# Key weight loads on ScalarE's queue, tile 0 in two halves, tiles 2 and 3 as two loads: one change at the start of a linear-attention and MLP kernel

## The chip, the cores and the metric

The kernel runs on one core of a Trainium2 chip. The metric is the device time of one execution in microseconds (us), the median over several executions. Engines are named as in the profile: PE is TensorE's matmul side and PEld its weight loads, DVE is VectorE, ACT is ScalarE, POOL is GpSimd, SP is SyncE. SPq, ACTq and POOLq are the sequencers of these engines, where waits and DMA issues are recorded.

## The reference: what is computed

The input x has 2048 tokens of 512 channels. It is normalised per token without scale or shift, and the result feeds two branches, which are added to x:

```
xn = (x - mean(x)) / sqrt(var(x) + 1e-5)            # per token, over 512 channels
q, k, v = xn @ wqkv, split in 3, 32 heads of 16     # wqkv is 512 x 1536
pq, pk = phi(q), phi(k)                             # phi(t) = (t + 1 if t > 0 else exp(t)) + 1e-6
kv = sum over tokens of pk^T v ;  z = sum over tokens of pk
o = (pq kv) / (pq . z + 1e-6)
h = relu(xn @ w1 + b1) ** 2                         # w1 is 512 x 1376
out = x + o @ wo + h @ w2 + b2
```

All data are float32. The kernel splits every operand of a product into a high part in a reduced float32 format (fp32r) and the rest, and adds three products (high by high, high by rest, rest by high), so each product of two matrices is three passes of matmuls.

## The kernel before: tiles, stages and order of the work

The 2048 tokens are 16 tiles of 128. The kernel is written with a hand-made schedule: the order of the instructions on each engine is the order in which the program text emits them. Each engine takes its own instructions in that order, and waits only on semaphores.

Three stages follow each other. First, for every tile, the tile is normalised, turned (channels onto partitions), split, and multiplied by the key part of wqkv; phi of that, multiplied by the tokens themselves, is added up over all tiles in four banks (`kx`, line 398). Then comes the queries' part with the small matrices made from that sum. Then the MLP, mixed with the rest of the attention, in two rounds of two blocks of 512 tokens.

The change touches the first few microseconds of stage one. What the code does there:

- Line 69 asks for ScalarE's table of functions (the table load). Lines 517 to 520 run 11 matmuls on a constant, which the profile shows as 22. They use no input.
- Lines 522 to 530 issue the loads, all on SP's queue, in this order: tile 0 (256 KB), tile 1 (256 KB), the four blocks of the key weights `rk` (256 KB each, `load_k`, line 527), and one load of tiles 2 and 3 together (512 KB).
- `statistics` and `measure` (lines 228 to 238) give mean and variance of a tile by `bn_stats` and `bn_aggr` on DVE. `roots` (lines 240 to 244) makes an estimate of the inverse root from a logarithm and an exponential on ACT. `normalise` (lines 246 to 276) refines it in three small instructions on DVE and writes the normalised tile `xp` (line 271).
- In DVE's order the statistics of tiles 0 and 1 both stand ahead of `normalise` of tile 0 (lines 568 to 578).
- `turned_pe` (line 318) transposes a tile by four matmuls; for tiles 0 and 1 the result lies in two halves. `high` (line 334, ACT) and `low` (line 337, DVE) split it into `xs1h` and `xs1l`.
- `heads_k` (line 560) copies a block of key weights into its high part `wkh` on ACT, and `rests_k` (line 564) makes the rest `wkl` on DVE or POOL. On ACT the order is: block 0, first half of tile 0's split, block 1, the other three halves, blocks 2 and 3.
- `some` and `rest` multiply tiles 0 and 1 by the key weights, a block at a time (lines 571 to 622); all of that is recorded at line 379. Tile 2 is measured, normalised and turned behind it (lines 606 to 620), and tile 3 is measured at line 617.
- Lines 586 and 587: a copy of one column on POOL into tile 4's buffer, from a result of tile 1's `normalise`, holds back the load of tiles 4 to 7 (1024 KB) until that result is there.

Of the kernel before, what the change touches and what calls it, by code (L numbers as in the profile page):

```python
# [13 lines left out]
P = 128  # L14
# [4 lines left out]
def kernel(  # L19
# [29 lines left out]
    nc = tc.nc  # L49
    xf = x.rearrange("b s d -> (b s) d")  # L50
    of = out.rearrange("b s d -> (b s) d")
    S, D = xf.shape
# [12 lines left out]
    FL = F - (NF - 1) * P  # L65
    Q = P // TB
    assert D == 512 and S % BT == 0 and FL == 3 * Q

    nc.scalar.preload_act_table_set("natural_log_exp_and_others")

    keep = ctx.enter_context(tc.tile_pool(name="keep", bufs=1))
    work = ctx.enter_context(tc.tile_pool(name="work", bufs=1))
# [12 lines left out]
    def next_tag(of):  # L85
        k, n = turns[of]
        turns[of][0] = (k + 1) % n
        return f"{of}{k}"

    def two(name):  # L90
        return keep.tile([P, 2, 512], F32, name=name, tag=next_tag("x"))

    def four(name, tag, dt=F32, pool=None):
        return (pool or work).tile([P, TB, 512], dt, name=name, tag=tag)
# [38 lines left out]
    def both(name, tags, dt=F32R, pool=keep):  # L133
        return [pool.tile([P, NJ, D], dt, name=f"{name}{u}", tag=t) for u, t in zip("hl", tags)]
# [18 lines left out]
    xr, xp, xg, tok, pk, kp = {}, {}, {}, {}, {}, {}  # L153

    def load_x(i, t):
        n = t.shape[1]
        nc.sync.dma_start(t, xf[i * P:(i + n) * P, :].rearrange("(i p) d -> p i d", i=n))  # L157
        for k in range(n):
            xr[i + k] = t[:, k]
# [6 lines left out]
    def chunk(w, j, a, b):  # L166

        return w[j * P:(j + 1) * P, a:b]
# [59 lines left out]
    def measure(g, *ks):  # L228

        tiles, st, mv, _ = g  # L230
        for k in ks or range(len(tiles)):
            nc.vector.bn_stats(st[:, k, :], xr[tiles[k]])
            nc.vector.bn_aggr(mv[:, k, :], st[:, k, :])

    def statistics(*tiles):
        g = group(*tiles)
        measure(g)
        return g
# [281 lines left out]
        nc.tensor.matmul(pw[:, :P], lhsT=zeros, rhs=zeros, start=True, stop=True)  # L520
    nc.vector.memset(eps, 1e-5)
    t, rk = two("x0"), four("rk", "r0")
    for i in range(2):
        load_x(i, t[:, i:i + 1])
    def load_k(*js):
        for j in js:
            nc.sync.dma_start(rk[:, j], chunk(wqkv, j, D, 2 * D))  # L527

    load_k(*range(NJ))
    load_x(2, two("x2"))  # L530
    nc.gpsimd.memset(ident, 0.0)
    nc.gpsimd.affine_select(out=ident, in_=ident, compare_op=OP.not_equal, fill=1.0, base=0,
                            pattern=[[-1, P]], channel_multiplier=1)
# [8 lines left out]
    for i0 in range(0, NT, TB):  # L542
# [5 lines left out]
        n = TB if i0 >= NPE else NPE - NDVE  # L548
        o = work.tile([P, n, 512], F32, name=f"xg{i0}", tag="r0" if i0 + TB == NT else "r3" if i0 >= NPE else "rc")
        for k in range(0, n, 2):  # L550
            i = i0 + TB - n + k
# [6 lines left out]
    def heads_k(*js, eng="act"):  # L558
        for j in js:
            copy(eng, wk[0][:, j, :], rk[:, j])  # L560
# [7 lines left out]
    two_tiles = statistics(0), statistics(1)  # L568
# [14 lines left out]
    normalise(*two_tiles[1])  # L583
    heads_k(1)

    nc.gpsimd.tensor_copy(x4[:, 0, :1], two_tiles[1][3][:, 2, :1])
    load_x(4, x4)
    low()
# [39 lines left out]
    soon = group(4, 6, 7)  # L628
    phi_k(0, pks[0])
    measure(soon, 0)  # L630
    tokens(0)
    parts(0)
    keep2()
    roots(*fourth)
    normalise(*fourth)
    phi_k(1, pks[1])
    measure(soon, 1)
    tokens(1)
    parts(1)
# [171 lines left out]
    m = both("m", ("mh", "ml"), pool=work)  # L811
# [25 lines left out]
    for n in range(2):  # L837
        t1, t2 = NB - 1 - 2 * n, NB - 2 - 2 * n
        x1, x2 = xsb
# [361 lines left out]
```

## Time and profile before

| what | value |
|---|---|
| median of the runs | 421.64 us (421.62 to 423.54, three runs) |
| the profiled execution's own time | 422.41 us |
| its span, first to last instruction | 420.7 us |
| PE busy | 414.1 us, 98% |
| DVE, ACT, POOL busy | 304.9, 253.0, 55.2 us |
| granted TensorE clock | 0.999 |

A row of the timeline gives the start, the duration, the engine, the line, the operation with output and inputs, and in brackets the idle time of the engine before it with what ended that idle time. Several like instructions in a row are merged into one row with their count. Matmuls are pipelined: one of 512 columns is shown with 0.39 us, while the next one starts 0.23 us after it.

### The profile page before, as it was taken

The numbers are of one execution on the slowest core, as the hardware profiler recorded it, in microseconds if no ns is written. First come the engines' busy times: TensorE is split into PE (matmuls) and PEld (weight loads), VectorE is DVE, ScalarE is ACT, GpSimd is POOL, SyncE is SP. The second block draws the span as 40 slices with busy tenths as digits, with TensorE's granted clock in tenths as the row PEclk, the third lists the DMA queues.
The fourth block names the chain that finished last, engine by engine and source line by source line (L and its number), as shares of the span: only waits on it lengthen the run. The fifth ranks groups of instructions, "written<-read, shape, count | busy, mean of one in ns | idle before, by whom it ended". The sixth has DMA issues, their size and how long they took to land.

```text
span 420.7 us, 5470 instructions
## 1 busy us (share of the span) xinstructions
PE 414.1 (98%) x1859; PEld 340.6 (81%) x1859; DVE 304.9 (72%) x555; ACT 253.0 (60%) x451; POOL 55.2 (13%) x78
## 2 busy tenths in 40 slices
PE   7999999999999999999999999999999999999996
PEld 6788888888887788888888887888788888888875
DVE  5995767786679987777579397586977667577293
ACT  5767777675467777565466371666677665546140
POOL 3231222220004000110000061001000200000240
PEclk9999999999999999999999999999999999999999
DMA  6885423800511322695026676501121784023742
GB/s 235 274 234 163 130 92 99 277 25 3 125 50 52 99 64 63 191 184 175 0 69 190 192 230 159 139 0 50 44 82 26 225 172 153 2 94 87 193 77 100
DMA packets 49485, 50.69 MB, mean 120 GB/s; under 512 B 8241, under 2 KB 33585, under 8 KB 49202
## 3 DMA queue, kind: packets, MB, share of 16 engines
q1 hardware_dynamic: 47154, 46.16, 36.4%
q0 software_dynamic: 2304, 4.20, 6.1%
q8 instruction: 14, 0.23, 0.3%
q14 instruction: 13, 0.11, 0.1%
HBM read 37.23 MB, written 8.91 MB: 110 GB/s over the span
## 4 chain that ended last, share of the span: by engine, by line
PE 96%; DMA 2%; DVE 1%; SPq 1%; issue 0%
PE acc L129 36%; PE b L489 23%; PE kx L398 10%; PE pq L379 10%; PE pk L379 9%; PE acc L500 2%; DMA x<-in_A_x_dram 2%; PE pz L129 1%; PE b L129 1%; PE pkv L820 1%; PE pm L129 1%; PE pt L318 0%; PE acc L507 0%; SPq L527 0%; SPq L157 0%; PE end L129 0%
## 5 line engine op out<-in xcount | busy, mean ns | idle before, releaser
L129 PE MATMUL acc<-w2r,s 128*128 128x512 f32 x477 | 112.8, 389 | 0.0
L129 PEld LDWEIGHTS acc<-w2r,s 128*128 128x128 f32 x477 | 89.5, 188 | 18.9 <-issue 0.2
L489 PE MATMUL b<-T,aop 128*128 128x512 f32 x240 | 59.9, 390 | 0.0
L489 PEld LDWEIGHTS b<-T,aop 128*128 128x128 f32 x240 | 44.8, 188 | 9.8 <-issue 0.5
L398 PE MATMUL kx<-pk,tok 128*128 128x512 f32 x192 | 46.8, 393 | 0.0
L398 PEld LDWEIGHTS kx<-pk,tok 128*128 128x128 f32 x192 | 35.6, 188 | 8.0 <-DVE pk L387 0.6
L956 POOL DMA_DIRECT2D res<-in_B_b_dram x16 | 14.1, 1067 | 150.5 <-DMA res<-in_A_x_dram 57.5
L121 DVE TENSOR_TENSOR w2r<-r,w2r 128x512 fp32r<-128x512 f32 (+2 forms) x35 | 25.4, 725 | 7.3 <-ACT w2r L110 7.2
L129 PE MATMUL acc<-mh,aTsr 128*128 128x512 f32 x96 | 30.6, 391 | 0.0
L118 POOL TENSOR_TENSOR tok<-xp,tok 128x512 fp32r<-128x512 f32 x16 | 21.7, 1363 | 54.8 <-ACT tok L110 54.8
L110 ACT ACTIVATE w2r<-r 128x512 fp32r<-128x512 f32 x32 | 20.0, 625 | 13.7 <-PE acc L129 11.3
L489 PE MATMUL b<-xs0h,aop 128*128 128x512 f32 x80 | 26.4, 391 | 0.0
L118 DVE TENSOR_TENSOR s<-c,s 128x512 fp32r<-128x512 f32 x20 | 13.8, 692 | 15.0 <-ACT s L110 14.9
L110 ACT ACTIVATE aop<-S 128x512 fp32r<-128x512 f32 x20 | 12.6, 629 | 16.1 <-DVE S L749 12.3
L374 DVE SCALAR_TENSOR_TENSOR q<-pq,q 128x512 f32<-128x512 f32 x16 | 11.0, 690 | 14.4 <-ACT q L372 14.4
L129 PEld LDWEIGHTS acc<-mh,aTsr 128*128 128x128 f32 x96 | 18.0, 188 | 4.0 <-issue 0.2
L370 ACT ACTIVATE q<-pq 128x512 f32<-128x512 f32 x16 | 9.4, 590 | 18.6 <-PE pq L379 18.5
L129 PE MATMUL acc<-ml,aTsr 128*128 128x512 f32 x48 | 18.7, 390 | 0.0
L964 DVE TENSOR_TENSOR res<-acc,res 128x512 f32<-128x512 f32 x16 | 11.0, 692 | 9.9 <-PE acc L129 6.6
L489 PEld LDWEIGHTS b<-xs0h,aop 128*128 128x128 f32 x80 | 15.0, 188 | 3.4 <-ACT rz L477 0.3
L303 DVE STREAM_TRANSPOSE at<-g 128x512 f32<-128x512 f32 x16 | 10.4, 689 | 7.9 <-DMA g<-q 7.9
L489 PE MATMUL b<-xs0l,aop 128*128 128x512 f32 x40 | 15.6, 390 | 0.0
(208 smaller groups left out, 854.9 us busy)
## 6 DMA issues: line engine op xcount, KB each, us to landing
r<-in_B_w_dram SPq DMA_DIRECT2D x49, 256.0 KB, 3.1
res<-in_A_x_dram SPq DMA_DIRECT2D x8, 512.0 KB, 5.8
res<-in_B_b_dram POOLq DMA_DIRECT2D x16, 256.0 KB, 5.3
g<-q SPq DMA_DIRECT2D x64, 64.0 KB, 2.5
out_dram<-res SPq DMA_DIRECT2D x15, 256.0 KB, 2.1
x<-in_A_x_dram SPq DMA_DIRECT2D x5, 512.0 KB, 6.0
via<-xp SPq DMA_DIRECT2D x5, 512.0 KB, 2.7
xg<-via SPq DMA_DIRECT2D x20, 128.0 KB, 2.9
```

The source lines that it names most:

```text
L110: nc.scalar.activation(o, i, AF.Copy, bias=bias)
L118: ENG[el].tensor_tensor(out=l, in0=src, in1=f32(h), op=OP.subtract)
L121: nc.vector.tensor_tensor(out=l, in0=src, in1=f32(h), op=OP.subtract)
L129: nc.tensor.matmul(ps, lhsT=a[u], rhs=b[v], start=first and n == 0, stop=last and n == 2)
L303: nc.vector.transpose(o.rearrange("p j (r t) -> p r j t", r=NJ), G.rearrange("p r (j c) -> p r j c", j=NJ))
L370: nc.scalar.activation(p, ps, AF.Relu, scale=-1.0)
L374: nc.vector.scalar_tensor_tensor(p, ps, 0.0, p, op0=OP.max, op1=OP.add)
L379: nc.tensor.matmul(ps, lhsT=cols(i)[u][:, j, slot(i)], rhs=w[v][:, j, :], start=first and n == 0, stop=last and n == len(steps) - 1)
L398: nc.tensor.matmul(kxp[c], lhsT=tok[i][:, u, c * P:(c + 1) * P], rhs=pk[i][:, v], start=i == 0 and (u, v) == first, stop=i == NT - 1 and ( ...
L489: nc.tensor.matmul(ps, lhsT=a[u][:, j * P:(j + 1) * P], rhs=b[v][:, j, :], start=first and j == 0 and n == 0, stop=last and j == 1 and n == 2,
L956: nc.gpsimd.dma_start(r[:, i], b2[None, :].partition_broadcast(P), accum_op=OP.add)
L964: nc.vector.tensor_tensor(out=r[:, a:z], in0=ps, in1=r[:, a:z], op=OP.add)
```

## The change

Four things are altered. Tile 0 is loaded by two loads, 256 of its 512 channels each, and its statistics are taken in two halves, which `bn_aggr` combines. Tile 2 is loaded alone, directly behind tile 1 on SP's queue. The four key weight loads are issued by ScalarE, behind the table load in its order; the call for the table load moves from the top of the function to that place. Tile 3 becomes a load of its own, held back by a second one-column copy on POOL in the same manner as tiles 4 to 7, and stands ahead of them on SP's queue. The `measure` helper is shared by all tiles; only tile 0 takes its branch with two halves.

```diff
-    nc.scalar.preload_act_table_set("natural_log_exp_and_others")
...
         for k in ks or range(len(tiles)):
-            nc.vector.bn_stats(st[:, k, :], xr[tiles[k]])
-            nc.vector.bn_aggr(mv[:, k, :], st[:, k, :])
+            n = 1 if tiles[k] else 2
+            for m in range(n):
+                nc.vector.bn_stats(st[:, k + m, :], xr[tiles[k]][:, m * D // n:(m + 1) * D // n])
+            nc.vector.bn_aggr(mv[:, k, :], st[:, k:k + n, :])
...
     t, rk = two("x0"), four("rk", "r0")
-    for i in range(2):
-        load_x(i, t[:, i:i + 1])
+    for k in range(2):
+        at = slice(k * D // 2, (k + 1) * D // 2)
+        nc.sync.dma_start(t[:, 0, at], xf[:P, at])
+    xr[0] = t[:, 0]
+    x2 = two("x2")
+    load_x(1, t[:, 1:])
+    load_x(2, x2[:, :1])
     def load_k(*js):
         for j in js:
-            nc.sync.dma_start(rk[:, j], chunk(wqkv, j, D, 2 * D))
+            nc.scalar.dma_start(rk[:, j], chunk(wqkv, j, D, 2 * D))
+    nc.scalar.preload_act_table_set("natural_log_exp_and_others")
     load_k(*range(NJ))
-    load_x(2, two("x2"))
...
     normalise(*two_tiles[1])
     heads_k(1)
 
+    nc.gpsimd.tensor_copy(x2[:, 1, :1], two_tiles[1][3][:, 2, :1])
+    load_x(3, x2[:, 1:])
     nc.gpsimd.tensor_copy(x4[:, 0, :1], two_tiles[1][3][:, 2, :1])
     load_x(4, x4)
```

## The prediction

> **What bounds the kernel now.** I read the page first, then the busy time by stretch, then the chain of work that ended last, and last the timeline of the first 13 us.
>
> ```profile
> span 420.7 us, 5470 instructions
> PE 414.1 (98%) x1859; PEld 340.6 (81%) x1859; DVE 304.9 (72%) x555; ACT 253.0 (60%) x451; POOL 55.2 (13%) x78
> ```
> ```profile
> 5.00:13.07 8.07, 5.92 (x28) 4.54 (x29) 6.82 (x23) 5.66 (x17) 1.65 (x4) 1.00 0.79 274
> 13.07:21.00 7.93, 7.92 (x38) 6.19 (x39) 7.03 (x16) 6.59 (x14) 2.65 (x4) 1.00 0.90 281
> 21.00:416.00 395.00, 395.00 (x1765) 324.93 (x1764) 288.20 (x512) 239.08 (x420) 49.34 (x63) 1.00 0.41 113
> ```
>
> The second fence gives, per stretch, its length and then the busy time of PE, PEld, DVE, ACT and POOL, the granted clock, the DMA share and GB/s. From 13.07 us on PE is never without work (395.00 of 395.00 us), at full clock. So a change to the start is worth exactly the shift of the moment from which PE runs unbroken, here the transposes of tile 2 at 13.07, as long as nothing later is made late. Ahead of it PE lacks 2.15 of 8.07 us. The chain shows what that moment hangs on:
>
> ```profile
> 3.62 6.65 DMA x<-in_A_x_dram
> ...
> 10.29 0.71 DVE st L232
> ...
> 13.07 0.63 PE pt L318 x4
> ```
> ```profile
> 8.35 0.40 PE L379 MATMUL pk<-wkh,xs1h 128*128 128x512 f32 x1
> ...
> 12.02 0.39 PE L379 MATMUL pk<-wkh,xs1h 128*128 128x512 f32 x1
> 12.25 0.39 PE L379 MATMUL pk<-wkh,xs1l 128*128 128x512 f32 x1
> 13.07 0.63 PE L318 MATMUL pt<-ident,xp 128*128 128x128 f32 x4 [0.44 <-DVE xp L271]
> ```
>
> The load of tiles 2 and 3 is issued seventh, lands 6.65 us later, and DVE measures tile 2 only then. Matmuls start 0.23 us apart (12.02, 12.25), so PE could have gone on at 12.48: the wait costs 13.07 - 12.48 = 0.59 us. That is all the gap at tile 2 can give back. The rest of the missing 2.15 us lies ahead of 8.35, where PE waits for tile 0 and the first key block:
>
> ```profile
> 0.81 1.28 ACT L69 ACT_TABLE_LOAD   x1 [0.81 <-PEq L1187]
> 0.81 0.87 SPq L157 DMA_DIRECT2D x<-in_A_x_dram  x2
> 1.72 1.85 SPq L527 DMA_DIRECT2D rk<-in_A_wqkv_dram  x4
> 3.59 0.69 DVE L232 BATCH_NORM_STATS2 st<-x 128x6 f32<-128x512 f32 x1 [2.65 <-DMA x<-in_A_x_dram]
> 4.32 0.18 DVE L233 BATCH_NORM_AGGREGATE mv<-st 128x2 f32<-128x6 f32 x1
> 4.42 0.66 DVE L232 BATCH_NORM_STATS2 st<-x 128x6 f32<-128x512 f32 x1
> 4.54 0.29 ACT L243 ACTIVATE y<-mv,eps 128x1 f32<-128x1 f32 x1 [2.45 <-DVE mv L233]
> 6.08 0.63 ACT L110 ACTIVATE wkh<-rk 128x512 fp32r<-128x512 f32 x1 [0.22 <-DMA rk<-in_A_wqkv_dram]
> 6.46 0.63 PE L318 MATMUL pt<-ident,xp 128*128 128x128 f32 x4 [1.52 <-DVE y L252]
> 6.90 0.39 ACT L334 ACTIVATE xs1h<-pt 128x256 fp32r<-128x256 f32 x1 [0.19 <-PE pt L318]
> 7.18 0.62 ACT L110 ACTIVATE wkh<-rk 128x512 fp32r<-128x512 f32 x1
> 8.51 1.09 DVE L337 TENSOR_TENSOR xs1l<-pt,xs1h 128x256 fp32r<-128x256 f32 x3 [0.17 <-ACT xs1h L334]
> ```
>
> ACT copies key block 0 at 6.08, when it lands; the first split of tile 0 stands behind that copy, at 6.90.
>
> **Part 1, tile 0 in halves.** Two issues for one, two statistics for one. One `bn_stats` of 512 takes 0.69; a half is an estimate of 0.42, since DVE's `xs1l` takes 1.09 for three of 256. Both loads' bytes are those of the one load, so I keep 3.56 us for the last of them. The second half is then measured by 4.0, not 4.28, and the aggregate is 0.27 earlier. It is not on the path: in DVE's order tile 1's statistics come before line 252, and tile 1 is now the third issue, not the second, 0.47 later.
>
> ```profile
> x<-in_A_x_dram SPq DMA_DIRECT2D x1, 256.0 KB, 2.8
> rk<-in_A_wqkv_dram SPq DMA_DIRECT2D x1, 256.0 KB, 4.3
> DMA to landing us min/median/max: 4.3/4.7/5.9
> x<-in_A_x_dram SPq DMA_DIRECT2D x1, 512.0 KB, 6.6
> x<-in_A_x_dram SPq DMA_DIRECT2D x1, 1024.0 KB, 7.1
> ```
>
> These rows are issue to landing: tile 0, key block 0, all four key blocks, tiles 2 and 3, and tiles 4 to 7. Tile 1, issued near 1.25, lands near 4.1 if it takes tile 0's 2.8; it waited then for tile 0's bytes more than for its issue. After, it lands between 4.1 and 4.6, and its statistics, at 4.42 before, start between 4.2 and 4.65. I take 4.42, the middle: 0 us, with -0.2 and +0.25 as ends.
>
> **Part 2, the key loads on ACT.** Four issues leave SP; ACT gets four. Nothing in this trace shows ACT issuing a load. The nearest row is SP's 0.43 per issue (1.85 for four with gaps); the far one is POOL's:
>
> ```profile
> L956 POOL DMA_DIRECT2D res<-in_B_b_dram x16: 844/940/1529, 176.9 to 401.0; - x16
> ```
>
> I take SP's, since these are plain loads as SP's are. If they start where the table load ends, 0.81 + 1.28 = 2.09, they go out at 2.13, 2.60, 3.08 and 3.55 and end near 4.0, ahead of the logarithm at 4.54: no cost on ACT. Block 0 is issued 2.13 - 1.72 = 0.41 later. With its own 4.3 us it lands near 6.45, its copy starts at 6.48, not 6.08, and ends at 7.11; the split of 6.90 moves to 7.13, the copy of 7.18 by as much. I charge PE +0.25 us at 8.35. Ends: nothing gained if the block comes earlier, since the split waits for the transposes until 6.90 anyway; with the longest of the four landings, 5.9, it lands at 8.03 and costs +1.75. I stay near the lower end because block 0's own row is the 4.3; the four rows grow with the bytes queued ahead. Blocks 2 and 3 land near 7.8 and 9.4 by their 4.7 and 5.9. The first is in time for its copy (8.90 + 0.25). The second is just in time for its own, some 0.55 later:
>
> ```profile
> 8.90 1.16 ACT L110 ACTIVATE wkh<-rk 128x512 fp32r<-128x512 f32 x2
> ```
>
> **Part 3, tile 2 alone behind tile 1.** Issued fourth on SP, near 2.2, it lands by 2.2 + 4.7 = 6.9, and even by 2.2 + 6.6 = 8.8 before DVE is free for it. DVE is free at 8.51 + 1.09 = 9.60, with part 2's shift 9.85, so its statistics start at 9.85, not 10.29. The chain to the transposes moves by 0.44: 12.63. PE's matmuls end their issue at 12.48 + 0.25 = 12.73, which is later, so PE goes on at 12.73 with no gap. 12.73 - 13.07 = **-0.34 us**. What is late next is PE's own work.
>
> **Part 4, tile 3 by itself.** One more copy on POOL (0.21 us) and one more issue on SP (0.43) ahead of tiles 4 to 7. Behind POOL's copies POOL next waits anyway; SP's next work is the store at 12.33.
>
> ```profile
> 7.19 0.21 POOL L586 COPY x<-y 128x1 f32<-128x1 f32 x1
> 8.34 0.10 POOL L356 MEMSET xp<- 128x1 f32 x1 [0.94 <-DVE wkl L564]
> 12.33 1.33 SPq L346 DMA_DIRECT2D xTd<-t  x2
> 13.45 0.69 DVE L232 BATCH_NORM_STATS2 st<-x 128x6 f32<-128x512 f32 x1
> 16.34 0.68 DVE L232 BATCH_NORM_STATS2 st<-x 128x6 f32<-128x512 f32 x1
> ```
>
> Tile 3 goes out near 7.5 and is measured at 13.45 - 0.44 = 13.0; 4.7 us would bring it at 12.2, 7.1 us only at 14.6, when DVE, with tile 2's split behind, would stall 1.6. The first is the nearer, a load of 256 KB: 0 us; the other end up to +0.6. Tiles 4 to 7 land 0.47 later than at 7.4 + 7.1 = 14.5, still ahead of their first use at 16.34. The second queue's effect outside the span (422.41 - 420.7 = 1.71 us) is shown by nothing; I take 0 and one issue, 0.43, either way.
>
> **Sum.** 0 (part 1) + 0.25 (part 2) - 0.59 (the gap of tile 2) + 0 (part 4) = -0.34 us, against the profiled execution's 422.41: 422.07. That execution stands 0.77 above the median, so from 421.64 I forecast 421.3 us. Its own range goes from -0.8 (gap gone, no key cost, tile 1 0.2 earlier) to -0.05 (tile 1 0.25 late, partly the same delay as the keys'): 420.8 to 421.6.
>
> **Rivals.** *The keys do not wait for the table load (slower).* ACT's sequencer can take up an instruction while ACT computes:
>
> ```profile
> 23.60 0.63 ACT L110 ACTIVATE pk<-k 128x512 fp32r<-128x512 f32 x1 [0.64 <-DVE k L374]
> L370 ACTq EVENT_SEMAPHORE  x1: 17/17/17, 23.6 to 23.6; - x1
> ```
>
> The wait for line 370 is handled at 23.6, the start of an activation of 0.63 us. If a load is taken up in the same way, the keys go out from 0.81 beside tile 0, and their bytes come between the tiles'. With one key block ahead of tile 1 it lands as third block of 256 KB, like key block 0 (1.72 + 4.3 = 6.0); with two, as fourth, like block 1 (2.20 + 4.5 = 6.7). Its statistics move from 4.42 to 6.0 or 6.7, and all behind them, and the 0.59 is still saved: +1.0 to +1.7, 422.6 to 423.4, in the middle 423.0. It decides against the change once tile 1 lands after 4.42 + 0.59 = 5.0. Against it: that row is a wait, not a load, and the instruction running is an activation, not the table load. By the Trainium skill, "Perfetto Trace Analysis", section Sequencer Loop, an engine instruction is pushed into a queue and control instructions are executed by the sequencer meanwhile, which speaks for this rival; the row agrees for waits, and no run here shows it for a table load.
>
> *The gain is eaten by the key blocks (no change).* Tile 2 now moves in the same microseconds as block 0. If block 0 takes the median 4.7 instead of 4.3, it lands at 6.83 and the split moves by 6.83 + 0.03 + 0.63 - 6.90 = 0.59: net 0, 421.6; up to +1.2 with 5.9. In that time tile 2 waits for nothing and PE stands ahead of 8.35 instead. By the Trainium skill, "DMA: Bandwidth & Descriptors", section Queues, rings and completion order, each DMA engine takes turns between queues a packet at a time, so two queues would share; the profile before has only one queue of this kind, so no row tells.
>
> *ACT's issue is as dear as POOL's.* At 1.07 us (the page's mean) four end at 2.09 + 4.28 = 6.37, the logarithm of tile 0 moves from 4.54 to 6.4: +1.85 - 0.59 = +1.3, 422.9.
>
> **How the numbers follow.** Forecast 0.45, keys beside tile 0 0.30, gain eaten 0.18, dear issue 0.05, anything else 0.02. The range 420.7 to 423.4 takes in the forecast's and both slower rivals' and leaves out their tails. A measurement of this kernel can tell about 0.5% (2.1 us) from no change: 419.5 and 423.75. Below the first only an unknown cause would lead, 0.02; above the second a third of the first rival (two key blocks ahead, with landings longer than before) and a little of the others, 0.13; the rest, 0.85, lies within.
>
> **What would show it.** ACT's issues at 2.1 to 4.0, behind the table load; tile 1's statistics at about 4.4; the copy of key block 0 near 6.5; tile 2's statistics near 9.9 without a wait for a load; no idle time of PE ahead of the transposes of tile 2, near 12.7; PE unbroken behind it. The forecast is wrong if key issues start near 0.8, if PE waits for tile 0's split beyond 7.7, or if DVE waits for tile 3 at 13.0.

## The result and the profile after

The changed kernel takes 426.0 us (425.17 to 426.21, six runs) against 421.79 for the kernel before beside it: the ratio is 1.0089, with a 95% interval of 1.0071 to 1.0107. It is 4.2 us slower. The forecast of 421.3, and its whole range, were wrong, and on the wrong side.

The profiled execution has a span of 424.3 us, 3.6 more than the one before. From the start of tile 2's transposes to the end it is 424.3 - 16.89 = 407.4 us, before 420.7 - 13.07 = 407.6. So the loss lies ahead of that point, as the prediction said it must. The first fence is the timeline of the changed kernel, the second its busy time by stretch: length, busy time of PE, PEld, DVE, ACT, POOL, granted clock, DMA share, GB/s.

```profile
0.80 1.28 ACT L536 ACT_TABLE_LOAD   x1 [0.80 <-PEq L1196]
0.83 1.84 ACTq L533 DMA_DIRECT2D rk<-in_A_wqkv_dram  x4
0.84 4.28 PE L520 MATMUL warm<-const-float32-0.0 128*128 128x128 f32 x22 [0.84 <-PEq L1196]
...
3.88 0.43 DVE L232 BATCH_NORM_STATS2 st<-x 128x6 f32<-128x256 f32 x1 [2.95 <-DMA x<-in_A_x_dram]
4.74 0.43 DVE L232 BATCH_NORM_STATS2 st<-x 128x6 f32<-128x256 f32 x1 [0.43 <-DMA x<-in_A_x_dram]
6.28 0.69 DVE L232 BATCH_NORM_STATS2 st<-x 128x6 f32<-128x512 f32 x1 [0.86 <-DMA x<-in_A_x_dram]
7.66 0.61 ACT L108 ACTIVATE wkh<-rk 128x512 fp32r<-128x512 f32 x1
8.35 1.09 PE L318 MATMUL pt<-ident,xp 128*128 128x128 f32 x4 [3.23 <-DVE y L252]
12.16 0.68 DVE L232 BATCH_NORM_STATS2 st<-x 128x6 f32<-128x512 f32 x1
12.64 0.63 PE L379 MATMUL pk<-wkh,xs1h 128*128 128x512 f32 x1
13.06 1.05 PE L379 MATMUL pk<-wkh,xs1l 128*128 128x512 f32 x2
15.07 0.39 PE L379 MATMUL pk<-wkh,xs1h 128*128 128x512 f32 x1
15.30 0.39 PE L379 MATMUL pk<-wkh,xs1l 128*128 128x512 f32 x1
16.89 0.60 PE L318 MATMUL pt<-ident,xp 128*128 128x128 f32 x4
```
```profile
6.00:7.00 1.00, 0.00 (x0) 0.00 (x0) 0.69 (x1) 0.00 (x0) 0.00 (x0) 1.00 1.04 397
7.00:8.00 1.00, 0.00 (x0) 0.00 (x0) 0.89 (x5) 0.75 (x3) 0.00 (x0) 0.79 0.19 68
8.00:9.00 1.00, 0.65 (x3) 0.68 (x4) 0.89 (x5) 0.27 (x1) 0.00 (x0) 0.50 0.00 0
13.00:14.00 1.00, 1.00 (x4) 0.74 (x3) 0.96 (x4) 0.87 (x4) 0.00 (x0) 0.50 1.07 416
14.00:15.00 1.00, 1.00 (x5) 0.81 (x4) 0.93 (x4) 0.72 (x3) 0.00 (x0) 0.80 0.76 293
15.00:16.00 1.00, 1.00 (x7) 0.80 (x6) 0.99 (x2) 0.00 (x0) 0.00 (x0) 1.00 0.48 134
```

Three things are to be seen. ScalarE issues the key loads at 0.83, inside its table load of 0.80 to 2.08, not behind it. Tile 1 is measured at 6.28 in place of 4.42, and the transposes of tile 0 start at 8.35 in place of 6.46: 1.89 us late. And PE, idle for 3.23 us, then works at half its pace until about 14.4: its matmuls start 0.42 us apart (12.64, 13.06), not 0.23 (15.07, 15.30), and the granted clock reads 0.50 up to 14 and 0.80 in the stretch behind it.

How tile 1 came to be late shows in the DMA issues, here one row for each issue up to tile 1's (issue to landing), without the second key block, for which no landing is recorded. The last two rows are what each queue moved up to 6.2 us: packets, MB and share of the DMA engines' time, q10 being ScalarE's queue and q1 SP's.

```profile
x<-in_A_x_dram SPq DMA_DIRECT2D x1, 128.0 KB, 3.1
rk<-in_A_wqkv_dram ACTq DMA_DIRECT2D x1, 256.0 KB, 3.3
x<-in_A_x_dram SPq DMA_DIRECT2D x1, 128.0 KB, 3.5
x<-in_A_x_dram SPq DMA_DIRECT2D x1, 256.0 KB, 4.5
```
```profile
q10 hardware_dynamic: 445, 0.82, 36.1%
q1 hardware_dynamic: 483, 0.63, 32.0%
```

The first half of tile 0 lands at 0.81 + 3.1 = 3.9, key block 0 at 0.83 + 3.3 = 4.1, the second half at 1.25 + 3.5 = 4.7, tile 1 at 1.72 + 4.5 = 6.2. Both queues advance together: by the time tile 1 has landed, the keys' queue has moved 0.82 MB, the bytes of three key blocks, beside the tiles' 0.63 MB. In the kernel before all loads together had moved 0.74 MB by 4.42 us, when tile 1 was being measured. The Trainium skill, "DMA: Bandwidth & Descriptors", section Queues, rings and completion order, says that a DMA engine goes round between its queues packet by packet; that both queues moved bytes all along agrees.

The time between the transposes of tiles 0 and 2 was 13.07 - 6.46 = 6.61 us before and is 16.89 - 8.35 = 8.54 now. The 0.59 us wait for tile 2 is gone (12.16 has no idle time before it), so the slow clock costs 8.54 - 6.61 + 0.59 = 2.5 us. The sum is 1.89 + 2.5 - 0.59 = 3.8, against a span that grew by 3.6. The execution profiled before took 0.77 us more than its kernel's median. Against the second profile of the kernel before (the last experiment: transposes at 6.55 and 12.55, span 420.1), which has no wait for tile 2, tile 0 is 1.80 us late and the slow pace costs 8.54 - 6.00 = 2.54. Together that is 4.3, and the span grew by 4.2, as the median did.

### The profile page after: what moved, and what is told of

It reads as the page before. It is cut to its first block, busy times and chain, and to the rows that moved or that the text cites. A ratio compares the mean times of both kernels' runs of the same rounds, so it can differ in the third digit from the quotient of the medians.

```text
span 424.3 us, 5476 instructions
## 1 busy us (share of the span) xinstructions
PE 416.8 (98%) x1859; PEld 342.8 (81%) x1859; DVE 305.2 (72%) x556; ACT 252.9 (60%) x451; POOL 55.0 (13%) x79
## 4 chain that ended last, share of the span: by engine, by line
PE 97%; DMA 1%; DVE 1%; SPq 0%; issue 0%; ACT 0%
PE acc L127 36%; PE b L489 23%; PE pk L379 11%; PE kx L398 10%; PE pq L379 10%; PE acc L500 2%; PE pz L127 1%; PE b L127 1%; DMA x<-in_A_x_dram 1%; PE pkv L829 1%; PE pt L318 1%; PE pm L127 1%; PE acc L507 0%; SPq L526 0%; PE end L127 0%; DVE st L232 0%
## 5 line engine op out<-in xcount | busy, mean ns | idle before, releaser
L374 DVE SCALAR_TENSOR_TENSOR q<-pq,q 128x512 f32<-128x512 f32 x16 | 11.0, 690 | 14.4 <-ACT q L372 14.4
```

What stands on the lines that cost most here:

```text
L374: nc.vector.scalar_tensor_tensor(p, ps, 0.0, p, op0=OP.max, op1=OP.add)
```

## The experiments

My theory after the result: the key loads' bytes make tile 1 late, and the idle time this opens halves PE's clock. The first four kernels try the two parts of that theory.

**More warm-up in the changed kernel.**

```diff
-    WARM = 11
+    WARM = 18
```

> The changed kernel with 18 warm-up matmuls in place of 11: TensorE has work until about 7.9 us and stands idle only about 0.5 us ahead of tile 0's transposes at 8.35. Theory (the key loads' bytes make tile 1 1.86 us late, and the long idle time that follows halves TensorE's clock, which costs another 2.5 us): granted clock 1.0 throughout, tile 2's transposes near 14.4 us in place of 16.89, about 423.5 us, 2.4 below the changed kernel. Rival (the slow stretch does not come from the idle time; it would be slow beside the loads in any case): no change, 426.

Measured: 423.7 us (423.4 to 424.13), ratio 1.0047 (1.0031 to 1.0064). Its timeline:

```profile
0.84 6.72 PE L520 MATMUL warm<-const-float32-0.0 128*128 128x128 f32 x36 [0.84 <-PEq L1196]
8.59 0.63 PE L318 MATMUL pt<-ident,xp 128*128 128x128 f32 x4 [1.03 <-DVE y L252]
14.59 0.60 PE L318 MATMUL pt<-ident,xp 128*128 128x128 f32 x4
```

The stretch between the transposes is 6.00 us, not 8.54, though tile 0's are as late as before. So the slow stretch does not come from the loads that run beside it but from what PE does ahead of the transposes, and it is worth 2.3 us of the 4.2 (426.0 - 423.7). The remaining 1.9 us are tile 1's lateness.

**Less warm-up in the kernel before.**

```diff
-    WARM = 11
+    WARM = 5
```

> The kernel before with 5 warm-up matmuls in place of 11, loads untouched: TensorE is idle from about 2.7 to 6.46 us, 3.8 us in place of 1.5. Theory (idle time of more than 3 us halves the clock): half clock for some microseconds, about 2.0 to 2.5 us longer, 424. Rival (the halved clock belongs to the changed loads): 421.7, as before.

Measured: 423.83 us (423.04 to 424.21), ratio 1.0047 (1.0032 to 1.0062). With the loads untouched, less warm-up costs 2.1 us. Rows of its timeline and of its busy time by stretch:

```profile
6.29 1.09 PE L318 MATMUL pt<-ident,xp 128*128 128x128 f32 x4 [2.97 <-DVE y L252]
9.30 0.63 PE L379 MATMUL pk<-wkh,xs1h 128*128 128x512 f32 x1
9.72 0.63 PE L379 MATMUL pk<-wkh,xs1l 128*128 128x512 f32 x1
```
```profile
9.00:10.00 1.00, 1.00 (x4) 0.81 (x3) 0.90 (x3) 1.00 (x4) 0.86 (x2) 1.00 0.62 190
```

The matmuls start 0.42 us apart, while the granted clock is given as 1.00. So in these records a full clock is no proof; the spacing of the matmuls is.

My theory named the wrong event here, though it had the right price. The first row below is this kernel's warm-up, the others are the changed kernel's, from 1.1 to 4.1 us and from 4.3 us on (one matmul stands in both): count, then the shortest, median and longest duration in ns.

```profile
L520 PE MATMUL warm<-const-float32-0.0 x10: 421/421/553, 0.8 to 2.9; 128*128 128x128 f32 x10
L520 PE MATMUL warm<-const-float32-0.0 x15: 378/421/553, 0.8 to 4.0; 128*128 128x128 f32 x15
L520 PE MATMUL warm<-const-float32-0.0 x8: 273/273/378, 4.0 to 4.8; 128*128 128x128 f32 x8
```

In the changed kernel the pace rose near 4.2, while the warm-up ran, and fell again behind the idle time. With 5 warm-ups all ten matmuls run at the slow pace, and so do the first ones behind the idle time: nothing shows that the pace had ever risen. This run therefore shows that the slow stretch needs no changed loads, but not that an idle time of 2.97 us ends a full pace.

**The key loads in the place that the forecast had given them.** The loads wait for a small activation behind the table load, which writes the first column of each key block (overwritten by the loads).

```diff
     nc.scalar.preload_act_table_set("natural_log_exp_and_others")
+    nc.scalar.activation(rk[:, :, 0], zeros[:, :NJ], AF.Copy)
     load_k(*range(NJ))
```

> The changed kernel with one small ScalarE activation, which writes the first column of each key block, between table load and key loads; the loads then cannot be issued before it has ended, near 2.4 us. Theory (all that failed is the place of the key loads in time): tile 1 is measured near 4.4, key block 0 lands near 6.6, tile 2 waits for nothing, no drop of the clock, 421.3 to 422.0. Rival (two queues sharing the DMA engines delay block 0 or tile 1 wherever they start): 422.5 or more.

Measured: 423.64 us (423.44 to 424.07), ratio 1.0046 (1.0031 to 1.0061). Timeline, and four stretches:

```profile
2.34 1.83 ACTq L533 DMA_DIRECT2D rk<-in_A_wqkv_dram  x4
5.20 0.69 DVE L232 BATCH_NORM_STATS2 st<-x 128x6 f32<-128x512 f32 x1 [1.11 <-DMA x<-in_A_x_dram]
7.28 0.93 PE L318 MATMUL pt<-ident,xp 128*128 128x128 f32 x4 [2.22 <-DVE y L252]
14.61 0.60 PE L318 MATMUL pt<-ident,xp 128*128 128x128 f32 x4
```
```profile
7.00:8.00 1.00, 0.72 (x4) 0.56 (x4) 0.89 (x5) 0.53 (x2) 0.00 (x0) 0.73 1.00 385
8.00:9.00 1.00, 0.95 (x3) 0.57 (x3) 0.93 (x3) 0.72 (x2) 0.34 (x3) 0.50 0.05 16
10.00:11.00 1.00, 1.00 (x4) 0.76 (x4) 1.00 (x4) 1.00 (x4) 1.00 (x2) 0.57 0.70 231
11.00:12.00 1.00, 1.00 (x6) 0.82 (x5) 0.97 (x4) 0.61 (x2) 0.36 (x1) 1.00 0.95 336
```

My theory fell here in part: the late issue alone doesn't mend it. From 2.34 on the key blocks still share the DMA engines with tile 1, which is measured at 5.20, not 4.42; PE is idle for 2.22 us, and the clock halves again. It is low for a shorter time: by the shares of 0.73 and 0.57 it falls near 7.46 and rises near 10.86, where the changed kernel's fell near 7.58 and rose near 14.40 (0.79 and 0.80). From tile 0's transposes to tile 2's it is 14.61 - 7.28 = 7.33 us, against 6.00 with 18 warm-ups, so the low clock costs 1.3 us here, not 2.5. Even with its premise granted the forecast would have missed by 2.3 us.

**Only the issuer changed, in the kernel before.**

```diff
-            nc.sync.dma_start(rk[:, j], chunk(wqkv, j, D, 2 * D))
+            nc.scalar.dma_start(rk[:, j], chunk(wqkv, j, D, 2 * D))
```

> The kernel before with only the issuer of the key loads changed, SP to ScalarE; tile 0 in one load and tiles 2 and 3 in one load as before. Theory: the issues start near 0.83, tile 1 is measured near 6 us, TensorE's idle time passes 3 us and its clock halves; about 425 to 426. Rival (the loss needs the halves of tile 0 or the early tile 2): below 423.

Measured: 424.45 us (423.21 to 425.62), ratio 1.0064 (1.0040 to 1.0088). The profiled execution, the one of 423.21, has tile 1 measured at 5.57, PE idle for 1.76 us and a full clock; the others, at 424.3 to 425.6, are 1.1 to 2.4 us longer, two of them with clock figures of 0.994 and 0.996. So the issuer alone makes most of the loss, but not all: tile 1 is 0.7 us earlier here than in the changed kernel. Some 0.25 us of it lies outside the span: the four executions take 1.9 to 2.0 us more than their spans, those of the kernel before beside them 1.7.

**The gated loads with the idle time filled.** The gated kernel with `WARM = 15`.

> The changed kernel with the key loads held until the table load and one small activation have ended, and 15 warm-up matmuls in place of 11, so that TensorE is idle for less than 1 us ahead of tile 0's transposes. Theory (with the key loads in their place two costs were left: tile 1 late by about 0.8 us from sharing the DMA engines with the key blocks, and the halved clock): no half clock, transposes of tile 0 near 7.3 and of tile 2 near 13.3, 421.9, within 0.1% of the kernel before. Rival (more is lost to the two queues than tile 1's lateness): 422.8 or more.

Measured: 422.85 us (421.96 to 423.39), ratio 1.0021 (1.0011 to 1.0030). That is the rival's figure, but not all of it is lost in the span: six of the ten executions take 1.85 to 2.9 us more than their spans, against 1.7 in the kernel before. The median span is 420.7 us, 0.7 above the kernel before's 420.0. Tile 1 is measured at 4.57 in this execution and the clock is full, but ACT waits for key block 0:

```profile
6.95 0.63 ACT L108 ACTIVATE wkh<-rk 128x512 fp32r<-128x512 f32 x1 [0.91 <-DMA rk<-in_A_wqkv_dram]
13.03 0.60 PE L318 MATMUL pt<-ident,xp 128*128 128x128 f32 x4
```

In one execution tile 1 pays for the sharing, in another block 0. The longer warm-up is worth 423.64 - 422.85 = 0.8 us here, and in the median span 421.95 - 420.7 = 1.25 us, about what the low clock cost the gated kernel. What makes the time outside the span longer isn't known.

**One queue, in the order that the change wants.** The changed kernel with `load_k` on SP again and tile 2 between the key blocks.

```diff
-            nc.scalar.dma_start(rk[:, j], chunk(wqkv, j, D, 2 * D))
+            nc.sync.dma_start(rk[:, j], chunk(wqkv, j, D, 2 * D))
...
-    load_x(2, x2[:, :1])
...
-    load_k(*range(NJ))
+    load_k(0, 1)
+    load_x(2, x2[:, :1])
+    load_k(2, 3)
```

> The changed kernel with the key loads back on SP's queue and tile 2 between them: the two halves of tile 0, tile 1, key blocks 0 and 1, tile 2, key blocks 2 and 3; tile 3 held back as in the change. Theory (in one queue the bytes come in the order of issue, so tile 1 is no later than its extra issue, and tile 2's wait goes): tile 1 measured between 4.4 and 4.7, tile 2's transposes near 12.6 to 12.9, 421.2 to 421.5. Rival (the halves of tile 0 cost more than their issue): 422 or more.

**The same with tile 0 in one load.** The kernel before with that order of loads and with tile 3 held back as in the change.

```diff
-    load_k(*range(NJ))
-    load_x(2, two("x2"))
+    x2 = two("x2")
+    load_k(0, 1)
+    load_x(2, x2[:, :1])
+    load_k(2, 3)
...
+    nc.gpsimd.tensor_copy(x2[:, 1, :1], two_tiles[1][3][:, 2, :1])
+    load_x(3, x2[:, 1:])
     nc.gpsimd.tensor_copy(x4[:, 0, :1], two_tiles[1][3][:, 2, :1])
```

> The kernel before with only the order of its loads changed: tiles 0 and 1, key blocks 0 and 1, tile 2, key blocks 2 and 3 on SP's queue, and tile 3 held back by a one-column copy as in the change; tile 0 stays one load. Theory (the wait for tile 2, 0.59 us, is all there is to gain, and it is gained without a second queue): tile 2's transposes near 12.5, 421.1. Rival (key block 2 or 3 is late instead and the wait only moves): 421.7, no change.

Measured: 423.14 us with the halves (421.72 to 424.16; ratio 1.0025, 1.0011 to 1.0039) and 421.56 without (421.33 to 423.03; ratio 1.000, 0.9991 to 1.0009). First the timeline with halves, then without:

```profile
4.54 0.69 DVE L232 BATCH_NORM_STATS2 st<-x 128x6 f32<-128x512 f32 x1 [0.48 <-DMA x<-in_A_x_dram]
6.61 0.63 PE L318 MATMUL pt<-ident,xp 128*128 128x128 f32 x4 [0.73 <-DVE y L252]
12.61 0.60 PE L318 MATMUL pt<-ident,xp 128*128 128x128 f32 x4
```
```profile
4.27 0.66 DVE L232 BATCH_NORM_STATS2 st<-x 128x6 f32<-128x512 f32 x1
6.31 0.63 PE L318 MATMUL pt<-ident,xp 128*128 128x128 f32 x4 [1.24 <-DVE y L252]
12.30 0.60 PE L318 MATMUL pt<-ident,xp 128*128 128x128 f32 x4
```

Tile 1, issued at 1.72 as in the changed kernel, is measured at 4.54 here, so its later issue alone doesn't explain 6.28. The halves cost 0.3 us in these two traces, as tile 1's one extra issue would, and the median moves by 1.6, because the times with halves fall into two groups: four of ten executions at 421.7 to 422.1, six at 423.1 to 424.2. For four of the six the granted clock is 0.995 or 0.996, which fits a slow stretch; their traces weren't seen. Without halves the order of loads gains nothing over the kernel before: the 0.59 us that I expected wasn't there to be had, which led to the last run below.

**A little less warm-up in the kernel before.** `WARM = 8`.

> The kernel before with 8 warm-up matmuls in place of 11, loads untouched: TensorE is idle some 2.3 us ahead of 6.46, between the 1.8 us that left the clock alone and the 3.0 us that halved it. Theory (the longer the idle time, the more executions have the halved clock): a spread of times, some near 421.7 and some 1 to 2 us above. Rival (only idle times above 3 us count): 421.7 in all.

Measured: 423.29 us (421.5 to 424.29), ratio 1.0036 (1.0021 to 1.0051): two of ten executions at 421.5 and 421.6, eight at 423.0 to 424.3. The profiled one has 1.67 us of idle time and full pace behind it, though all 16 of its warm-up matmuls ran at the slow pace; three of the longer ones have clock figures of 0.994 and 0.995. So the spread came as forecast. The longer ones weren't seen: their pace may have fallen, or have risen only later, as with 5 warm-ups.

**The changed kernel with tile 0 whole.**

```diff
-    for k in range(2):
-        at = slice(k * D // 2, (k + 1) * D // 2)
-        nc.sync.dma_start(t[:, 0, at], xf[:P, at])
-    xr[0] = t[:, 0]
+    load_x(0, t[:, :1])
...
-            n = 1 if tiles[k] else 2
+            n = 1
```

> The changed kernel with tile 0 loaded and measured whole again; all else as changed, the key loads issued by ScalarE from 0.83 on. Theory (of the 1.9 us by which tile 1 is late, a part comes from the halves, which put one more issue and one more turn of a key block ahead of it): tile 1 measured near 5.6 in place of 6.28, TensorE idle about 2 to 2.5 us, the clock halved in most executions, 424.5. Rival (the halves do not matter beside the two queues): tile 1 near 6.3, 426.

Measured: 424.24 us (422.55 to 425.47), ratio 1.0052 (1.0029 to 1.0075). Tile 1 is measured at 5.29, a whole microsecond ahead of the changed kernel's 6.28:

```profile
5.29 0.69 DVE L232 BATCH_NORM_STATS2 st<-x 128x6 f32<-128x512 f32 x1 [0.29 <-DMA x<-in_A_x_dram]
7.37 0.63 PE L318 MATMUL pt<-ident,xp 128*128 128x128 f32 x4 [1.49 <-DVE y L252]
```

What the halves change shows in the bytes: from 2.0 to 4.1 us SP's queue moved 0.24 MB with them, in 254 packets, and 0.40 MB without, in 213 larger ones; the keys' queue moved 0.37 and 0.29 MB. So with the halves the tiles' queue got a smaller part of the bytes, in smaller packets; that the size of the packets is the reason fits, but no run varies it alone. With 424.45 for the issuer alone and 426.0 for everything, the change's cost divides thus: ScalarE's issues about 2.7 us over the kernel before beside them (424.45 - 421.7), the early tile 2 and the late tile 3 nothing that shows (424.24, 0.2 less, with four and six executions that spread over 2.4 and 2.9 us), the halves 1.8 (426.0 - 424.24).

**A try at a better version.** One queue, tile 0 whole, tile 2 between the key blocks, and `WARM = 14`.

> The kernel with one queue, tile 0 whole and tile 2 loaded between the key blocks, with 14 warm-up matmuls in place of 11. Theory (the executions near 423 are those with the clock halved or with tile 2 late; both are excluded here): all executions within 421.2 to 421.9, median about 421.4. Rival (the spread has another cause): some executions above 422.3 as before.

Measured: 421.93 us (421.54 to 423.07), ratio 0.9997 (0.9984 to 1.0011). No gain, and four of twelve executions stay above 422.6. By the times the theory fell, but the spans tell more: all twelve lie between 419.8 and 420.3 us, where those of the kernel before beside them go from 419.9 to 422.6. The longer executions that the theory meant are gone. The four above 422.6 take 2.8 to 2.9 us more than their spans, the other eight 1.7; why the time outside the span grows, no run shows. In the profiled one the warm-up itself is in the way: its 28 matmuls take 6.18 us, and the transposes of tile 0 wait for them until 6.87.

```profile
0.85 6.18 PE L520 MATMUL warm<-const-float32-0.0 128*128 128x128 f32 x28 [0.85 <-PEq L1191]
6.87 0.60 PE L318 MATMUL pt<-ident,xp 128*128 128x128 f32 x4
```

**The kernel before, once more.** Nothing is edited.

> The kernel before, unaltered, for a second profile. Theory (the 0.59 us wait for tile 2 belongs to the one execution that was profiled first, 0.77 above the median): tile 2 is measured near 9.3 without a wait for its load, its transposes start near 12.3, about 421.6. Rival (the wait is there in every execution): transposes near 13.0.

Measured: 421.78 us. Tile 2 is measured with no idle time before it:

```profile
9.61 0.68 DVE L232 BATCH_NORM_STATS2 st<-x 128x6 f32<-128x512 f32 x1
12.55 0.60 PE L318 MATMUL pt<-ident,xp 128*128 128x128 f32 x4
```

The profile of `WARM = 8`, with the same loads, shows the same (9.33, 12.27). Of the four profiles with this order of loads (11 warm-ups twice, 8 and 5) only the one taken first has the wait of 0.59 us for tile 2.

## Why the prediction was wrong, point by point

The step that failed is the pair of terms for parts 1 and 2, 0 and +0.25 us, which assumed that key loads on a second queue leave the landing of tile 1 almost alone. In their place tile 0's transposes came 1.80 us late, because tile 1 did, and 2.54 us of slow matmuls followed, for which the sum had no term. The gain of 0.59 us, the third term, wasn't there.

- **What bounds the kernel: right.** After the transposes of tile 2 nothing moved (407.4 against 407.6 us); the whole loss lies ahead of them.
- **The term -0.59 of the sum: wrong.** The gap was real in the execution shown, which took 422.41, 0.77 above the median. The prediction stated that excess and subtracted it at the end, but didn't ask whether the gap was the excess. The second profile of the same kernel, at 421.78, has no gap, and the order of loads that removes it gains nothing in the median (421.56, ratio 1.000). Nothing was there to gain in a median execution.
- **Part 2, the issue at 2.13: wrong.** The first rival's start of the key loads was the right one, and it had 0.30. ACT's sequencer takes up a load 0.03 us after the table load has started, as it took up the wait at 23.6 in the quoted row, the only row that bore on the question. The rival's figure for tile 1, 6.0 or 6.7 against the measured 6.28, is right in part by luck. It counted three or four blocks of 256 KB up to tile 1; by 6.2 the two queues had moved 1.45 MB, over five, at 379 to 406 GB/s from 3 to 6 us, where the rows it took moved 254 to 311. The price of an issue (0.46 with gaps, 1.84 for four) was right.
- **Part 2, the key blocks' landing with an unchanged 4.3: wrong in its premise.** With the loads gated the first issue went out at 2.34, close to what was assumed, and either tile 1 (5.20) or block 0 (6.95) was late. Two queues share; the second rival named this, priced it for block 0 alone, and not for tile 1.
- **Part 1, the halves at 0: wrong in size.** In one queue they cost 0.3 us, near the end of +0.25 that was named, though the median moved by 1.6; beside a second queue they made tile 1 later by 1.0 us (6.28 against 5.29).
- **The term that was missing: the clock.** The first rival's own price, +1.0 to +1.7, is for tile 1's lateness alone, less the 0.59. PE's idle time was read only as time, though the 11 warm-up matmuls ahead of it stood in the code and in the profile as work that uses no input. 2.3 to 2.5 us of the 4.2 are this term.
- **Parts 3 and 4: right.** Tile 2 waited for no load in any kernel that loaded it early, and holding back tile 3 cost nothing that shows. Nothing was added outside the span either: the changed kernel's six executions take 1.67 to 1.75 us more than their spans, against 1.71.

What stays open: why some executions of the kernels with a short idle time stand 1 us or more above the rest. Two things are mixed there. In the kernel with one queue and 14 warm-ups the excess lies outside the span; in the kernel before it lies within (421.5 to 422.6 in three of 19 spans), and those traces weren't seen. The long executions of the kernel with 8 warm-ups and of those with tile 0 in halves weren't seen either; that they are slow stretches is inferred from their times and the clock figures of some. Three of the six executions of the changed kernel read 0.998 or 0.999, as the kernel with 5 warm-ups does, so the pace there may have been low from the start instead of falling; their times are much the same.

## What to carry to other kernels

Idle time of TensorE at the start is to be priced twice, once as time and once as a slow stretch behind it, when warm-up work has been put there: ask of each edit how long it leaves PE idle. A load moved to a second queue takes its turn with the first from its first byte on; where the order of landing matters, one queue kept it here. A gap in a single profile is a gain only if that execution's time is the median's, and a time should be split into its span and the rest before a cause is sought in the trace.

## What the runs showed of the hardware

- In two profiles the pace of PE rose in the warm-up and fell behind the idle time: in the changed kernel (risen near 4.2, idle for 3.23 us, low from 7.58 to 14.40) and in the gated one (risen near 4.0, idle for 2.22 us, low from 7.46 to 10.86). Both falls come 3.4 us after the rise, and the low stretches last 6.8 and 3.4 us. In the gated one the fall comes after PE has started again at 7.28. Behind idle times of 1.03 to 1.52 us a risen pace stayed (four profiles with the warm-up's end at the fast pace). The Trainium skill, "TensorE: Matmul & The Clock Gate", Part 1, describes a window of about 3.4 us that runs freely, not from the kernel's start. The steps of 3.4 us and the varying outcome fit that; a drop after 2.22 us of idle time is less than one such window.
- A warm-up can end before the pace rises. In four profiles (the issuer alone, one queue with halves, tile 0 whole in the changed kernel, 8 warm-ups) every warm-up matmul ran at the slow pace, 421 ns in the median, and the transposes behind an idle time of 0.73 to 1.76 us ran at the full one. With 5 warm-ups the pace was still low behind 2.97 us.
- The same 22 warm-up matmuls took 4.09, 4.28, 4.60 and 5.03 us in four profiles. They begin at a slower pace (starts 0.21 us apart, later 0.11), and the moment at which it ends varies; so the idle time behind them varies too.
- The mean granted clock of a run can read 0.999 with matmuls at half pace (the kernel with 5 warm-ups, 1.00 from 9 to 10 us); it also reads 1.00 while the warm-up matmuls of the changed kernel run at the slow pace. Two of the six executions of the changed kernel read 0.999 and took as long as the others.
- A load on ScalarE is issued while its table load runs: 0.83 inside 0.80 to 2.08. The Trainium skill, "Perfetto Trace Analysis", section Sequencer Loop, has an engine instruction pushed into a queue and a control instruction started by the sequencer itself. The trace agrees, if a load's issue counts as the second kind, which the section doesn't say.
